# The last token pair of a fused attention and ReGLU kernel: half tiles stored as they complete, and the last product copied by two engines

## The chip, the cores and the metric

The kernel runs on 1 core of one Trainium2 chip, as one program. The metric is the device time of that program in microseconds; lower is better. A change of time is read from medians of several runs.

## The reference

Sigmoid attention (no softmax) over 8 batches, 12 heads, 448 tokens and 64 dimensions is followed by a gated feed-forward layer over the 3584 tokens. The model width is 768, the hidden width 1536, and inputs and output are float32:

```python
def _attn_ref(q, k, v):
    S = q.shape[2]
    scale = 1.0 / np.sqrt(q.shape[-1])
    scores = scale * np.matmul(q, k.transpose(0, 1, 3, 2)) - np.log(S)
    attn = 1.0 / (1.0 + np.exp(-scores))
    return np.matmul(attn, v).astype(np.float32)

def _moe_ref(x, w_gate, w_val, w_out):
    gate = np.maximum(x @ w_gate, 0.0)
    val = x @ w_val
    return (gate * val @ w_out).astype(np.float32)

# x is attention's output with the heads side by side: (8 * 448, 768)
```

## The kernel before

The work is in float16 with float32 accumulation. Batches are taken in pairs (four groups g of two batches, 896 tokens each). The attention of one batch runs between pieces of the feed-forward layer of earlier batches; behind the last batch, the rest of the last group's feed-forward layer stands alone. It ends with the down projection, hidden 1536 to width 768.

The order of the instructions on each engine is the order of the program text (`manual_schedule`). The framework puts in the semaphores between engines. A queue issues in order: an instruction that waits holds up all that stand behind it on the same engine, DMA issues included.

The down projection takes the 896 tokens of a group as seven tiles of 128. One tile goes through `down`, plainly; the other six go in three pairs through `down_pair`. A pair's 256 x 1536 by 1536 x 768 product is treated as a 2 x 2 block product and worked out with seven block products of Strassen's kind instead of eight. `product` is one of them: six matmuls of 128 x 128 by 128 x 384 that sum up in one accumulator tile. There are three accumulator tiles for a pair, b (named "u" in the profile), c ("y12") and a ("y11"), and b takes four of the seven products, one after the other or added to what it holds.

Each product is read by one engine. `scaled_act` copies it on ScalarE (line 421), times OUT_SCALE; `scaled` does that on VectorE (line 416); `plus` adds it, scaled, to what an output tile holds, on VectorE (line 437). The outputs are two SBUF tiles of 128 tokens x 768 float32, y1 and y2 ("ysb"), each with a left half `lo` (columns 0 to 383) and a right half `hi` (384 to 767). HM is 384 and DM is 768.

`store` writes columns m0 to m1 of such a tile to the output, in two DMAs of 64 rows, since the 64-row halves of a tile belong to different chunks of tokens; `engines` names the queue that issues each. Line 339 is the DMA issue. A DMA of all 768 columns carries 192 KB, one of a half tile 96 KB. Only SyncE and ScalarE issue stores, and SyncE does no other work in this stage.

In the last pair (`last`), the order behind the fourth product is: y1's left half is summed; y2's right half is summed; y1's right half is summed; y1 is stored, its first 64 rows by SyncE and its second by ScalarE; the seventh product is made; ScalarE copies it to y2's left half; then y2's right half is stored by SyncE (two DMAs), and its left half by SyncE and ScalarE. The last `scaled_act` and ScalarE's store of y1 are on the same queue, with the store first. `then` has no work left to prepare at that point.

Of the kernel before, what the change touches and what calls it, by code (L numbers as in the profile page):

```python
# [12 lines left out]
AOP = mybir.AluOpType  # L13
AF = mybir.ActivationFunctionType
# [3 lines left out]
def kernel(  # L18
# [10 lines left out]
    nc = tc.nc  # L29

    B, H, S, D = q.shape
    DM, DF = moe_w_gate.shape
# [13 lines left out]
    OUT_SCALE = 1.0 / (XSCALE * XSCALE)  # L46
# [29 lines left out]
    def bank(name, shape=(P, 512), dtype=FP32):  # L76
        pool, tag = free[0]
        free.rotate(-1)
        return pool.tile(list(shape), dtype, tag=tag, name=name)
# [4 lines left out]
    def later(order):  # L84
        keys = [free[i - 8] for i in order]
        for key in keys:
            free.remove(key)
            free.append(key)
# [245 lines left out]
    def store(g, t, ysb, m0, m1, engines):  # L334
        for i, eng in enumerate(engines):
            j = 2 * t + i
            b, c = 2 * g + j // NCH, j % NCH
            dst = out[b * S : (b + 1) * S, m0:m1].rearrange("(t c) m -> c t m", c=NCH)[c]
            eng.dma_start(dst, ysb[64 * i : 64 * i + 64, m0:m1])
# [24 lines left out]
    HF, HM, HD = NFC // 2, DM // 2, NDC // 2  # L364
# [17 lines left out]
    def products(jobs):  # L382
        for ps, n, kn, A, W, first in jobs:
            for k_ in range(kn):
                nc.tensor.matmul(  # L385
                    ps[:, 0:n],
                    A[:, k_, :],
                    W[:, k_, :],
                    start=(first and k_ == 0),
                    stop=(k_ == kn - 1),  # L390
                    skip_group_check=True,
                )
# [8 lines left out]
    def token_blocks(g, p):  # L401
        h = hT_tiles[g]
        t1, t2 = (slice(t * P, (t + 1) * P) for t in (2 * p, 2 * p + 1))
        return h[:, 0:HF, t1], h[:, HF:NFC, t1], h[:, 0:HF, t2], h[:, HF:NFC, t2]
# [15 lines left out]
    def scaled_act(o, ps):  # L420
        nc.scalar.activation(o, ps[:, 0:HM], AF.Copy, scale=OUT_SCALE)  # L421

    def down_pair(g, p, beside, then, last, first_copy):
        A11, A12, S3, A22 = token_blocks(g, p)
        S1, S2, S4 = sums.pop(("y", g, p))
        T1, T2, T3, T4 = (late["T"][:, i] for i in range(4))
        B11, B21, B22 = wo[:, 0:HF, 0:HM], wo[:, HF:NFC, 0:HM], wo[:, HF:NFC, HM:DM]
        y1, y2 = (ysbp.tile([P, DM], FP32, tag="ysb", name="ysb") for _ in range(2))
        lo, hi = slice(0, HM), slice(HM, DM)
        b, c, a = bank("u"), bank("y12"), bank("y11")  # L430
        later((7, 6, 5))

        def product(ps, A, W, first=True):
            products([(ps, HM, HF, A, W, first)])

        def plus(o, ps):
            nc.vector.scalar_tensor_tensor(  # L437
                out=o, in0=ps[:, 0:HM], scalar=OUT_SCALE, in1=o, op0=AOP.mult, op1=AOP.add
            )

        product(b, A11, B11)
        first_copy(y1[:, lo], b)
        beside()
        product(c, S1, T1)
        scaled_act(y2[:, hi], c)
        product(b, S2, T2, False)
        scaled_act(y1[:, hi], b)
        product(a, A12, B21)
        plus(y1[:, lo], a)
        product(b, S3, T3, False)  # L450
        plus(y2[:, hi], b)
        product(c, S4, B22, False)
        plus(y1[:, hi], c)
        if last:
            store(g, 2 * p, y1, 0, DM, (nc.sync, nc.scalar))
        else:
            store(g, 2 * p, y1, 0, DM, (nc.sync, nc.sync))
        then()
        product(b, A22, T4, False)
        scaled_act(y2[:, lo], b)  # L460
        if last:
            store(g, 2 * p + 1, y2, HM, DM, (nc.sync, nc.sync))
            store(g, 2 * p + 1, y2, 0, HM, (nc.sync, nc.scalar))
        else:
            store(g, 2 * p + 1, y2, 0, DM, (nc.sync, nc.sync))


# [199 lines left out]
    def next_work(jobs=(), alone=False):  # L667
        kind, g, i = work.popleft()

        def beside():  # L670
            for job in jobs:
                job()

        if kind == "y":
            down_pair(g, i, beside, prepare, not work, scaled_act if alone else scaled)
        elif kind == "w":
            gv_pair(g, i, lambda: (prepare(), beside()), nc.scalar.copy if alone else nc.vector.tensor_copy)
        else:
            beside()
            prepare()  # L680
            down(g, i)
# [113 lines left out]
```

## Time and profile before

| what | us |
|---|---|
| median of 3 runs | 401.06 (400.89 to 401.36) |
| span of the profiled execution, first to last instruction | 399.2 |
| median of the runs less that span | 1.9 |
| TensorE busy, in the profiled execution | 388.9 (97% of the span) |
| VectorE busy | 279.9 (70%) |
| ScalarE busy | 223.0 (56%) |
| end of the last product, by the timeline | 393.84 |
| issue of the last store, by the timeline | 395.72 |

The profile is one execution; its own time is known by its span, and what lies around the span is taken from the median of the runs. Times in the views are microseconds from the start of the span. PE is TensorE, DVE is VectorE, ACT is ScalarE, SP is SyncE; a q behind an engine's name is its queue's own work, such as issuing a DMA. A row of the timeline gives start, duration, engine, line, operation and what it writes and reads. The time of a DMA issue is that in which the queue is taken; the time to landing runs from the start of the issue to the moment when all of its bytes have been confirmed.

### The profile page before, as it was taken

Reading aid. Unit: us, or ns where it says so; the run is one execution under the profiler, and the core shown is the slowest. Engines: PE = TensorE matmul, PEld = TensorE weight load, DVE = VectorE, ACT = ScalarE, POOL = GpSimd, SP = SyncE. Lnnn points to the kernel's source line nnn. Section 1 sums busy time; section 2 is a strip of 40 time slices with the busy share of each in tenths; the row PEclk is TensorE's granted clock in tenths of the full one; section 3 lists DMA queues with packets and bytes.
Section 4 is the critical chain, followed back from the end, with each engine's and each line's share of the span. In section 5 each row is a group of like instructions: output and inputs, shape, how many; then the busy total and the mean of one; then the engine's idle time right before and its main releaser. Section 6 shows DMA issues by size and latency. Waiting matters only on the chain.

```text
span 399.2 us, 8737 instructions
## 1 busy us (share of the span) xinstructions
PE 388.9 (97%) x3488; PEld 217.9 (55%) x3488; DVE 279.9 (70%) x539; ACT 223.0 (56%) x475; POOL 49.4 (12%) x73
## 2 busy tenths in 40 slices
PE   8999999999998999999999999999999999999994
PEld 3678786545455554554555555455455555555562
DVE  2454344367358889999758889999766779887661
ACT  5946778783885565655665455565566234533131
POOL 8643301600030300003000300000000000000000
PEclk9999999999999999999999999999999999999999
DMA  9999994999897894224945695223012320000144
GB/s 149 199 199 204 205 141 94 177 203 187 178 161 152 165 204 76 46 48 51 178 85 133 130 218 89 48 24 61 12 40 80 80 79 2 0 2 0 39 115 124
DMA packets 68793, 43.69 MB, mean 109 GB/s; under 512 B 35856, under 2 KB 65296, under 8 KB 68752
## 3 DMA queue, kind: packets, MB, share of 16 engines
q0 software_dynamic: 30736, 23.33, 39.1%
q1 hardware_dynamic: 37584, 19.24, 23.0%
q8 instruction: 27, 0.44, 0.5%
q10 hardware_dynamic: 432, 0.56, 0.4%
q14 instruction: 14, 0.11, 0.1%
HBM read 47.19 MB, written 11.01 MB: 146 GB/s over the span
## 4 chain that ended last, share of the span: by engine, by line
PE 73%; DMA 14%; issue 6%; POOL 3%; DVE 2%; ACT 1%; ACTq 0%; POOLq 0%; DVEq 0%
PE u L385 32%; PE g L385 15%; PE y L385 9%; DMA v<-in_v_dram 6%; PE qk_ps L232 5%; PE pv_ps L250 5%; DMA wo<-in_moe_w_out_dram 4%; DMA k<-in_k_dram 4%; PE ya L346 3%; PE v_ps L309 1%; PE yb L346 1%; PE g_ps L309 1%; POOL q L110 1%; POOL k L110 1%; DVE wv L376 1%
## 5 line engine op out<-in xcount | busy, mean ns | idle before, releaser
L187 ACT ACTIVATE PT<-qk_ps 128x448 f16<-128x448 f32 (+3 forms) x318 | 150.6, 594 | 71.2 <-PE qk_ps L232 71.1
L385 PEld LDWEIGHTS <-S 128*128 128x128 f16 x540 | 52.8, 98 | 44.4 <-issue 0.8
L528 DVE TENSOR_TENSOR gsb<-g,gsb 128x448 f32<-128x448 f32 x72 | 43.0, 625 | 14.5 <-PE g L385 13.8
L232 PE MATMUL qk_ps<-qkT 64*64 64x448 f16 (+2 forms) x756 | 50.0, 336 | 0.9 <-DVE qkT L206 0.5
L421 ACT ACTIVATE ysb<-u 128x384 f32<-128x384 f32 x27 | 13.4, 498 | 56.3 <-PE u L385 56.3
L327 DVE TENSOR_TENSOR hT<-gate_sb,v_ps 128x256 f16<-128x256 f32 (+2 forms) x36 | 16.2, 465 | 33.5 <-ACT gate_sb L318 22.4
L385 PEld LDWEIGHTS <-hT 128*128 128x128 f16 x288 | 27.7, 98 | 21.0 <-issue 3.2
L524 ACT COPY gsb<-u 128x448 f32<-128x448 f32 x48 | 25.8, 566 | 23.9 <-PE u L385 22.9
L250 PE MATMUL pv_ps<-PT,v 64*64 64x448 f16 (+2 forms) x756 | 37.4, 329 | 0.4 <-issue 0.4
L184 DVE TENSOR_SCALAR xT<-pv_ps 128x448 f16<-128x448 f32 (+2 forms) x53 | 27.9, 567 | 13.4 <-PE pv_ps L250 12.1
L232 PEld LDWEIGHTS <-qkT 64*64 64x64 f16 x756 | 20.3, 105 | 24.9 <-issue 16.3
L309 PE MATMUL v_ps<-xT,wv 128*128 128x256 f16 (+2 forms) x216 | 33.3, 291 | 0.4 <-DVE hT L327 0.2
L309 PE MATMUL g_ps<-xT,wg 128*128 128x256 f16 (+2 forms) x216 | 33.5, 292 | 0.1
L385 PEld LDWEIGHTS <-wv 128*128 128x128 f16 x216 | 21.1, 98 | 19.8
L385 PEld LDWEIGHTS <-wg 128*128 128x128 f16 x216 | 20.3, 98 | 20.6 <-issue 3.0
L250 PEld LDWEIGHTS <-v 64*64 64x64 f16 x756 | 21.8, 107 | 11.8 <-issue 1.4
L385 PE MATMUL u<-T,hT 128*128 128x384 f16 x144 | 27.3, 326 | 0.0
L437 DVE SCALAR_TENSOR_TENSOR ysb<-y,ysb 128x384 f32<-128x384 f32 x24 | 13.4, 557 | 18.8 <-PE y L385 11.3
L110 POOL DMA_DIRECT2D k<-in_k_dram x14 | 10.9, 779 | 112.3 <-DVE rel L215 105.8
L309 PEld LDWEIGHTS <-wg 128*128 128x128 f16 x216 | 18.5, 98 | 11.5 <-issue 5.0
L309 PEld LDWEIGHTS <-wv 128*128 128x128 f16 x216 | 20.1, 98 | 8.2 <-DMA wv<-in_moe_w_val_dram 0.5
L385 PE MATMUL u<-xT,wg 128*128 128x448 f16 x108 | 23.5, 353 | 0.1
(67 smaller groups left out, 531.3 us busy)
## 6 DMA issues: line engine op xcount, KB each, us to landing
out_dram<-ysb SPq DMA_DIRECT2D x53, 192.0 KB, 2.9
k<-in_k_dram POOLq DMA_DIRECT2D x5, 672.0 KB, 11.8
q<-in_q_dram POOLq DMA_DIRECT2D x5, 672.0 KB, 14.9
v<-in_v_dram POOLq DMA_DIRECT2D x8, 336.0 KB, 15.6
v<-in_v_dram POOLq DMA_DIRECT2D x16, 168.0 KB, 15.3
k<-in_k_dram POOLq DMA_DIRECT2D x8, 224.0 KB, 10.4
wo<-in_moe_w_out_dram POOLq DMA_DIRECT2D x1, 1536.0 KB, 13.2
q<-in_q_dram POOLq DMA_DIRECT2D x6, 224.0 KB, 11.3
```

What stands on the lines that cost most here:

```text
L110: nc.gpsimd.dma_start(t16[:, xs, cs], rows_of(src, b)[:, xs, cs])
L184: nc.vector.tensor_scalar(out=xT, in0=src, scalar1=XSCALE, scalar2=None, op0=AOP.mult)
L187: nc.scalar.activation(PT_ap, ps_ap, AF.Sigmoid, bias=sig_bias, scale=qk_scale)
L232: nc.tensor.matmul(out_of(hh)[o : o + 64, :], qkT[rows, c, cols], qkT[rows, NCH + c0 : NCH + c1, cols], start=True, stop=True, tile_positi ...
L250: nc.tensor.matmul(ps[hh][64 * r : 64 * r + 64, 0:qn], v16[rows, 2 * g + hh, c * D : (c + 1) * D], pieces[c][rows, hh, :], start=(c == 0), ...
L309: nc.tensor.matmul(ps[-1][:, 0:qn], wt[:, dc, f * P : (f + 1) * P], xT_tiles[b][:, dc, q0 : q0 + qn], start=(dc == 0), stop=(dc == NDC - 1),)
L327: nc.vector.tensor_tensor(out=hT_tiles[g][:, f, o : o + qn], in0=gate_sb[:, 0:qn], in1=ps[1][:, 0:qn], op=AOP.mult,)
L346: nc.tensor.matmul(ps[:, 0 : m1 - m0], hT_tiles[g][:, f, t * P : (t + 1) * P], wo[:, f, m0:m1], start=(f == 0), stop=(f == NFC - 1),)
L385: nc.tensor.matmul(ps[:, 0:n], A[:, k_, :], W[:, k_, :], start=(first and k_ == 0), stop=(k_ == kn - 1), skip_group_check=True,)
L421: nc.scalar.activation(o, ps[:, 0:HM], AF.Copy, scale=OUT_SCALE)
L524: by(gs[u][i][:], ps[u][:, 0:S])
L528: nc.vector.tensor_tensor(out=gs[u][i][:], in0=ps[u][:, 0:S], in1=gs[u][i][:], op=AOP.add)
```

## The change

In the last pair alone, three things change. Each half of y1 and the right half of y2 is stored right behind the `plus` that completes it: y1's left half and y2's right half by SyncE, y1's right half by SyncE and ScalarE. The stores of the last pair become eight of 96 KB, six on SyncE and two on ScalarE; before they were two of 192 KB and four of 96 KB. And the seventh product's 384 columns are copied as two quarters of the output tile, columns 0 to 191 by ScalarE and 192 to 383 by VectorE. Nothing else is changed.

```diff
         product(a, A12, B21)
         plus(y1[:, lo], a)
+        if last:
+            store(g, 2 * p, y1, 0, HM, (nc.sync, nc.sync))
         product(b, S3, T3, False)
         plus(y2[:, hi], b)
+        if last:
+            store(g, 2 * p + 1, y2, HM, DM, (nc.sync, nc.sync))
         product(c, S4, B22, False)
         plus(y1[:, hi], c)
         if last:
-            store(g, 2 * p, y1, 0, DM, (nc.sync, nc.scalar))
+            store(g, 2 * p, y1, HM, DM, (nc.sync, nc.scalar))
         else:
             store(g, 2 * p, y1, 0, DM, (nc.sync, nc.sync))
         then()
         product(b, A22, T4, False)
-        scaled_act(y2[:, lo], b)
         if last:
-            store(g, 2 * p + 1, y2, HM, DM, (nc.sync, nc.sync))
+            q3 = slice(0, HM // 2), slice(HM // 2, HM)
+            nc.scalar.activation(y2[:, q3[0]], b[:, q3[0]], AF.Copy, scale=OUT_SCALE)
+            nc.vector.tensor_scalar(
+                out=y2[:, q3[1]], in0=b[:, q3[1]], scalar1=OUT_SCALE, scalar2=None, op0=AOP.mult
+            )
             store(g, 2 * p + 1, y2, 0, HM, (nc.sync, nc.scalar))
         else:
+            scaled_act(y2[:, lo], b)
             store(g, 2 * p + 1, y2, 0, DM, (nc.sync, nc.sync))
```

## The prediction

> **What bounds the kernel now.** I read the page first, for the bound of the whole span.
>
> ```profile
> span 399.2 us, 8737 instructions
> PE 388.9 (97%) x3488; PEld 217.9 (55%) x3488; DVE 279.9 (70%) x539; ACT 223.0 (56%) x475; POOL 49.4 (12%) x73
> ```
>
> TensorE is busy for 97% of the span, and the diff touches none of its instructions. What can move lies behind the last matmul. The chain of waits, asked for the last microseconds, shows what that is (start us, us, what):
>
> ```profile
> 391.89 0.99 PE y L385 x6
> ...
> 392.98 0.57 DVE ysb L437
> ...
> 393.56 0.55 ACTq L339
> 394.11 0.05 issue
> 394.16 0.49 ACT ysb L421
> ```
>
> The last product runs beside the DVE row (the timeline has it from 392.70 to 393.84). ScalarE could then copy it, but it issues a store first (393.56, 0.55 us), so its copy runs from 394.16 to 394.65. The chain stops at that copy; the span goes on to 399.2. So next I read the timeline of SyncE in narrow windows, one store in each:
>
> ```profile
> 393.56 0.47 SPq L339 DMA_DIRECT2D out_dram<-ysb  x1
> 394.07 0.60 SPq L339 DMA_DIRECT2D out_dram<-ysb  x1
> 394.71 0.91 SPq L339 DMA_DIRECT2D out_dram<-ysb  x1
> 395.72 0.54 SPq L339 DMA_DIRECT2D out_dram<-ysb  x1
> ```
>
> This is the bound of the tail. Four stores stand in a row on one queue: one half of the token rows of y1, two of the right half of y2 (complete since 392.54, as DVE's row at 391.99 of 0.56 us says), and the last product's. The copy was done at 394.65, and the last store waits 1.07 us more for its turn. ScalarE's own last store starts at 394.68. The DMA view from 391.0 to 399.2 tells what follows (40 slices of 0.205 us; then KB of each store and us to landing, where the 3.1 is a median):
>
> ```profile
> DMA  0000000000000000028998799899787940000000
> out_dram<-ysb SPq DMA_DIRECT2D x3, 96.0 KB, 3.1
> out_dram<-ysb SPq DMA_DIRECT2D x1, 192.0 KB, 2.7
> out_dram<-ysb ACTq DMA_DIRECT2D x1, 192.0 KB, 3.4
> out_dram<-ysb ACTq DMA_DIRECT2D x1, 96.0 KB, 2.8
> ```
>
> Asked store by store, the three 96 KB ones of SyncE take 3.1, 3.2 and 2.4 us in that order. So the last lands at 395.72 + 2.4 = 398.1, and the span ends 1.1 us behind it, with the program's closing steps. Bytes move from about 394.6 (1.1 us after the first issue) to 397.7 (0.4 us ahead of the last landing). SyncE's store before these was issued by 389.1 (388.53, 0.60 us); from there to 393.56 its queue stands empty, though y1's left half is complete at 391.57 (DVE's row at 391.01, 0.56 us).
>
> The median of the runs is 401.06 us, the profiled span 399.2. I carry the 1.9 us between them unchanged and set the sum against the landing at 398.1.
>
> **The change part by part.**
>
> *Early stores.* Six issues on SyncE replace four, all of 96 KB. Their price on that queue is the issue time. The nearest rows are the four stores of an earlier pair, which stand in one burst:
>
> ```profile
> 379.91 0.47 SPq L339 DMA_DIRECT2D out_dram<-ysb  x1
> 380.42 0.60 SPq L339 DMA_DIRECT2D out_dram<-ysb  x1
> 381.12 0.55 SPq L339 DMA_DIRECT2D out_dram<-ysb  x1
> 381.71 0.59 SPq L339 DMA_DIRECT2D out_dram<-ysb  x1
> ```
>
> With the gaps between them that is about 0.6 us a store; before's 96 KB ones took 0.60, 0.91 and 0.54, so the size does not shorten the issue. Laid end to end: y1 left at 391.59 and 392.10 (queue free at 392.70); y2 right, complete at 392.54, at 392.80 and 393.39 (free at 393.99); y1 right, complete at 393.54, at 394.08 (free at 394.63). Two issues are added, 1.2 us, and they cost nothing while the matmuls to 393.84 and the copies behind them cover them. Without that cover they would push the last store back by 1.2 us. So four of the six are issued by 394.0, and only y1's right half stands ahead of the last store. That one moves from 393.56 to 394.08 on this queue, and only the end of the program waits for it.
>
> *ScalarE's queue.* It still issues y1's store first (half of it), waiting for the same DVE row. I take 0.55 us again, so its copy still starts at 394.16. Between bounds: SyncE issues at the same time, and where both queues issued at once, one store took 0.91 instead of about 0.55. At worst the copy starts 0.36 us later; as ScalarE's two issues measured 0.55 and 0.50 beside a busy SyncE, I take none of it.
>
> *The split copy.* The durations are in the groups by shape, on the same engines:
>
> ```profile
> L318 ACT ACTIVATE gate_sb<-g_ps 128x192 f32<-128x192 f32 x12 | 3.9, 388 | 4.3 <-PE g_ps L309 4.3
> L184 DVE TENSOR_SCALAR xT<-pv_ps 128x192 f16<-128x192 f32 x6 | 1.9, 353 | 2.1 <-PE pv_ps L250 2.1
> ```
>
> The ScalarE mean is 388 ns in a crowded stretch, and one alone at 53.89 takes 0.33 us. As the 128x384 copy is 0.49 in the tail and 0.50 on average, I take 0.33: ScalarE ends at 394.49. For VectorE I take 0.35. It is free from 393.54, and it starts 0.1 us after a matmul's end (391.99 after 391.89), so side by side it would run from 393.94 to 394.29 and cost nothing. The other bound is one after the other: both halves lie in one accumulator tile, and VectorE then starts at about 394.53 and ends at 394.88. The trace does not tell: in the code each product has exactly one reader, so no row has two engines in one bank. I take one after the other, as all rows do, with the ends kept: copies complete at 394.49 or 394.88, where before it was 394.65. Taken so, the split alone is a loss of 0.23 us. The Trainium skill ("PSUM — Partial Sum Buffer", section "PSUM bank collisions raise a hardware error") speaks against this edit: two engines must not be in the same bank and quadrant at once, two readers included, and software has to order them. By that rule the copies end at 394.88, without it at 394.49, and no run here shows a collision.
>
> *The last stores.* VectorE's half makes both of them wait for two engines. Nothing is queued behind either but the closing steps. SyncE is free at 394.63, so both issue at about 394.91: SyncE's 0.81 us earlier than 395.72, ScalarE's 0.23 us later than 394.68. Now SyncE's turn no longer decides, the copies do.
>
> *The landing.* The rows for 96 KB are 2.4 to 3.2 us. The two high ones had two or more stores waiting ahead of them. Of the lowest, 2.4, some was still waiting: a store that waits for nothing has 1.1 us to its first bytes, about 0.4 us of bytes (two slices) and 0.4 us to the landing, 1.9 us. The highest that I allow for is ScalarE's 2.8, with another queue's stores ahead of it. As two stores start together and y1's may still be moving, I take 2.4, and 1.9 to 2.8 as bounds.
>
> *The sum.* 394.91 + 2.4 = 397.31 against 398.1: 0.8 us. The closing steps stay, 1.1 us. SyncE begins them with short waits, one landing after another (L790's rows show eleven of 28 ns in all); up to 0.1 us of them may already be done when the last store lands, and I count 0.05. Together 0.85 us, 401.06 - 0.85 = 400.2 us. The bounds of this case: 1.9 us gives 396.8, a gain of 1.3 (399.75); 2.8 us and ScalarE's copy 0.36 late gives 398.1, no gain (401.05).
>
> **The rivals.**
>
> *Side by side indeed.* The copies end at 394.49; SyncE's queue is then the bound with 394.68, landing 397.1, a gain of 1.0 and 400.0 us; with the 1.9 us landing 1.5, 399.55. For it: VectorE has nothing to do from 393.54. Against: no row shows it.
>
> *The DMA engines hold the tail.* Eight groups of 64 rows replace six with the same bytes. If each takes 0.6 us as on the issuing queue, bytes from 391.59 + 1.1 = 392.7 end at 397.5, the landing is 397.9 and the gain 0.2: 400.85 us. For it: halving the bytes from 192 to 96 KB did not shorten an issue. Against: in before six stores moved from 394.6 to 397.7, 0.52 each, and eight of those end at 396.8.
>
> *Writes wait for the stores (slower).* Each tile is now read by a store while its other half is still to be written. If that write is made to wait until the store has landed, VectorE's last sum of y1 waits at 392.98 for the second store, 392.10 + 3.1 = 395.2. VectorE ends at 395.8, ScalarE issues to 396.4, copies to 396.75 (y2's stores, from 393.39 + 3.1 = 396.5, hold it no longer than that), VectorE's half follows to 397.1, stores land at 397.15 + 2.4 = 399.55: 1.45 us later than 398.1, 402.5 us. It decides once VectorE's sum starts over 0.8 us late, at about 393.8. Against it: before's store of y2's right half started at 394.07, while ScalarE wrote the left half of that tile from 394.16 to 394.65, so halves are told apart in that direction. The opposite direction has no row.
>
> **How the numbers follow.** A change of 0.2%, 0.8 us, is about what a measurement of this kernel can tell from none. My forecast case (copies in turn, stores early) has 0.62; its centre, 0.85, lies just over that mark, so 0.34 of it is faster and 0.28 the same. Side by side has 0.16, all faster. The DMA engines' case has 0.13, the same. Waiting writes have 0.09: 0.07 slower, and 0.02 the same where the wait is short. Together 0.50 faster, 0.43 same, 0.07 slower. The range goes from the lower end of side by side (399.6) to no gain (401.1); what it leaves out is mostly the waiting writes. The forecast case alone has 399.75 to 401.05.
>
> **What would show it.** Right: SyncE stores from 391.6 on with no gap until 394.6; the last pair of stores at about 394.9, landing near 397.3; VectorE's 128x192 row starting only when ScalarE's ends. Wrong: VectorE's row at 393.94 (side by side), a landing time of the last stores of 3 us (the DMA engines), VectorE's sum L437 later than 393.0 or a ScalarE issue of 0.9 us.

## The result and the profile after

| | us |
|---|---|
| before, median of 9 runs | 401.06 (400.78 to 401.75) |
| changed, median of 9 runs | 400.35 (399.83 to 401.10) |
| ratio, 95% interval | 0.9978 [0.9969, 0.9987] |
| predicted | 400.2 (399.6 to 401.1) |

The changed kernel is faster by 0.22%, with the interval from 0.13% to 0.31%. The chain of waits of the changed kernel, in its last microseconds (start us, us, what):

```profile
393.80 0.55 ACTq L339
394.35 0.05 issue
394.40 0.34 ACT ysb L466
394.74 0.02 issue
394.76 0.36 DVE ysb L467
```

ScalarE still issues its store of y1 first, and its copy starts when that is done. VectorE's quarter (L467) starts when ScalarE's has ended. The two copies stand one behind the other.

SyncE's timeline, in narrow windows with one store in each:

```profile
391.83 0.47 SPq L339 DMA_DIRECT2D out_dram<-ysb  x1
392.34 0.60 SPq L339 DMA_DIRECT2D out_dram<-ysb  x1
393.03 0.55 SPq L339 DMA_DIRECT2D out_dram<-ysb  x1
393.63 0.60 SPq L339 DMA_DIRECT2D out_dram<-ysb  x1
394.33 0.54 SPq L339 DMA_DIRECT2D out_dram<-ysb  x1
395.14 0.47 SPq L339 DMA_DIRECT2D out_dram<-ysb  x1
```

In before the queue was taken from 393.56 to 396.26 with four stores in a row. Now five of the six stores are issued by 394.87, and from there the queue is free until both quarters are copied, at 395.12. The DMA view from 391.0 to 398.6 (40 slices of 0.19 us), and the last two stores asked for alone:

```profile
DMA  7000000000696299188549698892789810000000
out_dram<-ysb SPq DMA_DIRECT2D x1, 96.0 KB, 2.2
out_dram<-ysb ACTq DMA_DIRECT2D x1, 96.0 KB, 2.4
```

The first slice still shows the stores ahead of the last pair. The last pair's bytes move from 393.0 on, so while the last product is being made, and they end at about 397.2.

One thing has to be taken out before two single executions are compared. The diff touches nothing ahead of the last pair, yet the last product ends at 393.84 in the profile of before and at 394.07 in this one; in all profiles of this case that end lies between 393.65 and 394.78. This scatter is larger than the effect. What the change does is therefore read from the last product's end to the end of the span: 5.31 us in before, 4.45 us here, 0.86 us less.

### The profile page after: what moved, and what is told of

It is laid out like the page before. It is cut to its first block, busy times and chain, and to the rows that moved or that the text cites. A ratio compares the mean times of both kernels' runs of the same rounds, so it can differ in the third digit from the quotient of the medians.

```text
span 398.5 us, 8744 instructions
## 1 busy us (share of the span) xinstructions
PE 388.5 (97%) x3488; PEld 217.6 (55%) x3488; DVE 280.2 (70%) x540; ACT 222.9 (56%) x475; POOL 49.5 (12%) x73
## 4 chain that ended last, share of the span: by engine, by line
PE 84%; DMA 10%; POOL 2%; DVE 2%; ACT 1%; issue 1%; ACTq 0%; POOLq 0%; DVEq 0%
PE u L385 32%; PE g L385 15%; PE y L385 9%; PE qk_ps L232 7%; PE pv_ps L250 7%; DMA wg<-in_moe_w_gate_dram 6%; PE g_ps L309 5%; PE v_ps L309 5%; DMA v<-in_v_dram 4%; PE ya L346 3%; PE yb L346 1%; POOL q L110 1%; ACT PT L187 1%; DVE wv L376 1%; POOL k L110 1%
```

## The experiments

The theory: in before, SyncE's turn decided when the last store was issued; the early stores empty that queue and bring the gain; the split copy is a small loss, since its halves follow one another. The first rival: the split brings the gain. The second: the DMA engines' pace, not the issue, sets the last landing.

All times of this table are counted from the end of the last product, from the trace. "Issue" is the start of the last store on ScalarE's and on SyncE's queue, "landing" the later landing of the two, "end" the end of the span. Each row's times are of one execution; the two executions of the changed kernel, and the two of e6, agree within 0.03 us.

| kernel | issue ScalarE, SyncE | landing | end | ratio to before, 95% interval |
|---|---|---|---|---|
| before | 0.84, 1.88 | 4.27 | 5.31 | 1 |
| changed | 1.08, 1.07 | 3.49 | 4.45 | 0.9978 [0.9969, 0.9987] |
| after_again | 1.07, 1.07 | 3.46 | 4.42 | 0.9985 [0.9977, 0.9994] |
| e1_early_only | 0.84, 0.89 | 3.44 | 4.34 | 0.9982 [0.9973, 0.9992] |
| e2_split_only | 1.08, 1.88 | 4.54 | 5.57 | 1.0008 [1.0000, 1.0017] |
| e3_y2_first | 0.83, 0.83 | 3.85 | 4.96 | 0.9996 [0.9987, 1.0005] |
| e4_eight_late | 0.84, 1.57 | 3.87 | 4.77 | 0.9990 [0.9981, 0.9998] |
| e5_dve_copy | 0.63, 0.89 | 3.37 | 4.28 | 0.9977 [0.9967, 0.9988] |
| e6_two_queues | 0.63, 0.62 | 3.00 | 3.99 | 0.9962 [0.9949, 0.9976] |
| e6_again | 0.63, 0.62 | 3.00 | 3.97 | 0.9961 [0.9948, 0.9974] |
| e7_vector_first | 0.79, 0.89 | 3.30 | 4.20 | 0.9966 [0.9953, 0.9980] |
| e8_by_rows | 1.43, 0.89 | 3.54 | 4.44 | 0.9979 [0.9970, 0.9988] |
| e9_hi_first | 0.84, 3.00 | 5.16 | 6.06 | 1.0016 [1.0006, 1.0026] |
| e10_two_queues_scalar | 0.79, 0.78 | 3.16 | 4.15 | 0.9974 [0.9964, 0.9984] |

The difference in "end", divided by 401, agrees with every ratio to within its interval (changed: 0.86 / 401 = 0.21%; e9: 0.74 / 401 = 0.18% slower). The intervals are 0.17% wide or wider, which is 0.7 us; where two kernels lie closer than that, the ratios hardly part them, and the comparison rests on single traces.

**The changed kernel again**, on the chip of the next three:

> The changed kernel once more on the same chip, as the measure for the others: ratio to before 0.998, last stores 1.07 us after the last product's end, last landing 2.4 us later.

The same tail to within 0.04 us; the ratio's interval reaches 0.9994 and overlaps the first one. Over both measurements the gain is 0.15 to 0.22%.

**One part alone: the early stores.** The diff is against the changed kernel.

```diff
-            q3 = slice(0, HM // 2), slice(HM // 2, HM)
-            nc.scalar.activation(y2[:, q3[0]], b[:, q3[0]], AF.Copy, scale=OUT_SCALE)
-            nc.vector.tensor_scalar(
-                out=y2[:, q3[1]], in0=b[:, q3[1]], scalar1=OUT_SCALE, scalar2=None, op0=AOP.mult
-            )
+            scaled_act(y2[:, lo], b)
```

> The stores of the change, but ScalarE alone copies the last product (384 columns, 0.49 us). Theory (SyncE's queue was the bound, and the split is a loss because its halves run one after the other): the copy ends about 0.2 us earlier than in the changed kernel, both last stores issue about 0.8 us after the end of the last product instead of 1.07, and the time is 0.2 us below the changed kernel's: a ratio to before of about 0.9973. Rival 'the split brings the gain': the time falls back towards before, ratio 1.000. Rival 'the DMA engines hold the tail': the last landing does not move although the last stores issue earlier, ratio equal to the changed kernel's, 0.998.

The tail keeps all of its gain without the split (4.34 us), so the first rival is out. The last stores issue when the theory said, 0.2 us ahead of the changed kernel, but the landing comes only 0.01 to 0.05 us earlier; the rest of the 0.08 to 0.11 us at the end is in the closing steps (0.90 us instead of 0.96). SyncE's last store now takes 2.56 us instead of 2.17. The last two stores, asked for alone:

```profile
out_dram<-ysb ACTq DMA_DIRECT2D x1, 96.0 KB, 2.4
out_dram<-ysb SPq DMA_DIRECT2D x1, 96.0 KB, 2.6
```

So the second rival has a part in it; e8 and e10 below take that up.

**The other part alone: the split copy**, with before's stores in before's order.

```diff
-        scaled_act(y2[:, lo], b)
         if last:
+            q3 = slice(0, HM // 2), slice(HM // 2, HM)
+            nc.scalar.activation(y2[:, q3[0]], b[:, q3[0]], AF.Copy, scale=OUT_SCALE)
+            nc.vector.tensor_scalar(
+                out=y2[:, q3[1]], in0=b[:, q3[1]], scalar1=OUT_SCALE, scalar2=None, op0=AOP.mult
+            )
             store(g, 2 * p + 1, y2, HM, DM, (nc.sync, nc.sync))
             store(g, 2 * p + 1, y2, 0, HM, (nc.sync, nc.scalar))
         else:
+            scaled_act(y2[:, lo], b)
```

> The split copy alone; the stores are those of before, in before's order. Theory: nothing is gained, since SyncE's last store comes to its turn about 1.88 us behind the last product's end either way; ScalarE's last store is 0.2 us later and lands before SyncE's. Ratio 1.000, within 0.0005; VectorE's row starts when ScalarE's has ended. Rival 'the split brings the gain': ratio 0.998, with both rows at the same time.

SyncE's last store issues at 1.88 us, as before, so the split gains nothing. It even loses 0.26 us, which I had not expected. SyncE's timeline, and the landing of that one store:

```profile
396.27 0.59 SPq L339 DMA_DIRECT2D out_dram<-ysb  x1
out_dram<-ysb SPq DMA_DIRECT2D x1, 96.0 KB, 2.7
```

In before the same store took 2.4 us. ScalarE's store, 0.24 us later than in before because of the serial copies, now moves its bytes closer to SyncE's last ones (it lands at 4.18 instead of 3.60 us behind the product). That the two get in each other's way is what the times suggest; it was not tried by itself.

**Order of the queue alone.** Six stores as in before, but y2's right half goes ahead of y1, which is stored whole; ScalarE copies the last product whole.

```diff
         plus(y2[:, hi], b)
+        if last:
+            store(g, 2 * p + 1, y2, HM, DM, (nc.sync, nc.sync))
         product(c, S4, B22, False)
...
         if last:
-            store(g, 2 * p + 1, y2, HM, DM, (nc.sync, nc.sync))
             store(g, 2 * p + 1, y2, 0, HM, (nc.sync, nc.scalar))
```

> Only the order of the queue: y2's right half is stored when it is complete instead of behind y1, y1 is stored whole as before, ScalarE copies the last product whole. Six stores, as in before. Theory (turn on the queue): SyncE is free when the copy is done, the last stores issue about 0.8 us after the last product instead of 1.88, ratio 0.997 to 0.998. Rival 'the DMA engines hold the tail': y1's two 192 KB stores now move bytes up to the end, the last stores take 3 us or more to land and half of the gain is lost, ratio 0.9985 or above. Rival 'splitting y1 is what matters': ratio near 1.000.

The last stores issue at 0.83 us, 1.05 us earlier than in before, and yet the end comes only 0.36 us earlier. Their landings, asked for alone:

```profile
out_dram<-ysb SPq DMA_DIRECT2D x1, 96.0 KB, 2.8
out_dram<-ysb ACTq DMA_DIRECT2D x1, 96.0 KB, 3.0
```

Here the second rival holds. Y1's two stores of 192 KB are issued just ahead, land at 2.54 and 3.15 us behind the product, and the last ones queue behind them. Turning the queue round was not enough; y1's left half has to be away early as well.

**Y1 in halves, meant to be late.**

```diff
         if last:
-            store(g, 2 * p, y1, 0, DM, (nc.sync, nc.scalar))
+            store(g, 2 * p, y1, 0, HM, (nc.sync, nc.sync))
+            store(g, 2 * p, y1, HM, DM, (nc.sync, nc.scalar))
```

> Before with y1 stored in halves, but no earlier than before: two more issues stand on SyncE's queue in the tail, uncovered, and the bytes are the same. Theory (each issue costs its 0.6 us on the queue once nothing covers it): the last store issues about 1.2 us later than in before, ratio 1.002 to 1.003. Rival 'bytes set the tail': same bytes, same time, ratio 1.000.

The edit did not do what I meant. SyncE's timeline:

```profile
392.40 1.11 SPq L339 DMA_DIRECT2D out_dram<-ysb  x2
```

This is 2.25 us ahead of the last product's end (394.65 in this run). SyncE has no other work, so a store's place in the program text does not hold it; it issues as soon as its half tile is complete and the stores ahead of it on the same queue are gone. So this run is "y1's left half early, y2's right half still behind y1": 0.54 us of gain. With e3's 0.36 us for y2's order, and 0.97 us for both (e1), each early half has a share.

**The issues without cover.** The same stores with y1's right half ahead of its left one, so that SyncE has to wait for y1's last sum first:

```diff
         if last:
-            store(g, 2 * p, y1, 0, DM, (nc.sync, nc.scalar))
+            store(g, 2 * p, y1, HM, DM, (nc.sync, nc.scalar))
+            store(g, 2 * p, y1, 0, HM, (nc.sync, nc.sync))
```

> Before with y1 stored in halves, the right half first and the left half behind it, so that no store of the tail can issue before y1's last sum: eight stores, none of them covered by the last products, the bytes as in before. Theory (an issue costs its 0.6 us on SyncE's queue once nothing covers it): the last store issues 2.8 to 3.1 us behind the end of the last product instead of 1.88, and the span ends 6.2 to 6.5 us behind it instead of 5.3: ratio 1.002 to 1.003. Rival 'bytes set the tail': same bytes at the same time, 5.3 us, ratio 1.000.

```profile
397.50 0.55 SPq L339 DMA_DIRECT2D out_dram<-ysb  x1
out_dram<-ysb SPq DMA_DIRECT2D x1, 96.0 KB, 2.2
```

The last store issues 3.00 us behind the product (394.50 in this run), 1.12 us later than in before: the price of two issues that nothing covers, with the same bytes. Only 0.74 us of that reach the end (6.06 us, a little less than expected), since the store that is alone at the end lands in 2.2 instead of 2.4 us and the closing steps take 0.90 instead of 1.04. "Bytes alone set the tail" is out.

**Who orders the two copies.** First by rows instead of columns, 64 rows for each engine; the diff is against the changed kernel:

```diff
-            q3 = slice(0, HM // 2), slice(HM // 2, HM)
-            nc.scalar.activation(y2[:, q3[0]], b[:, q3[0]], AF.Copy, scale=OUT_SCALE)
-            nc.vector.tensor_scalar(
-                out=y2[:, q3[1]], in0=b[:, q3[1]], scalar1=OUT_SCALE, scalar2=None, op0=AOP.mult
-            )
+            nc.scalar.activation(y2[0:64, lo], b[0:64, 0:HM], AF.Copy, scale=OUT_SCALE)
+            nc.vector.tensor_scalar(
+                out=y2[64:P, lo], in0=b[64:P, 0:HM], scalar1=OUT_SCALE, scalar2=None, op0=AOP.mult
+            )
```

> The stores of the change; the last product is shared out by rows, 0 to 63 to ScalarE and 64 to 127 to VectorE, 384 columns each. If two engines are kept apart only where they share rows of the accumulator, VectorE runs from 0.1 to 0.65 us after the last product, beside ScalarE (0.3 to 0.8), and the last stores issue at 0.7 (ScalarE's queue) and 0.85 us: ratio 0.997. If they are kept apart by the accumulator as a whole, VectorE starts when ScalarE ends, at 0.85, and the last stores issue at 1.45 us: 0.4 us above the changed kernel, ratio 0.999.

```profile
394.95 0.48 ACT L465 ACTIVATE ysb<-u 64x384 f32<-64x384 f32 x1 [3.70 <-PE u L385]
395.47 0.56 DVE L466 TENSOR_SCALAR ysb<-u 64x384 f32<-64x384 f32 x1 [1.15 <-ACT ysb L465]
```

VectorE's 64 other rows wait for ScalarE all the same, and the row names ScalarE as what ended its wait. Half the rows take as long as all (0.48 and 0.56 us), so the copies end at 1.40 us. The time I expected for this case was wrong: SyncE's store only needs ScalarE's rows and issues at 0.89, and ScalarE's, issued at 1.43, lands in 2.11 us. The end is that of the changed kernel. The two copies share the accumulator and the output tile, and the row does not say which of them is guarded. The output tile is told apart by rows at least between a copy and a store: SyncE's store of rows 0 to 63 issues at 0.89, while VectorE writes rows 64 to 127 from 0.84 to 1.40. That points to the accumulator, but no run copies one accumulator to two output tiles.

The landings of e8's last two stores also bear on e1:

```profile
out_dram<-ysb SPq DMA_DIRECT2D x1, 96.0 KB, 2.3
out_dram<-ysb ACTq DMA_DIRECT2D x1, 96.0 KB, 2.1
```

SyncE's store has the same issue time as in e1, 0.89 us, and the same stores ahead of it on its queue. ScalarE's last store differs: it comes 0.54 us behind SyncE's here, and 0.05 us ahead of it in e1. SyncE's lands in 2.30 us here and in 2.56 us in e1. (In e7 and e5, where ScalarE's is 0.10 and 0.26 us ahead, it takes 2.41 and 2.48 us.) So some 0.26 us of e1's landing goes with ScalarE's store, started just ahead; the stores on SyncE's own queue, the same in both, do not explain it.

Then the two quarters in the opposite order of text:

> The change with the two quarter copies in the opposite order of text, VectorE's first. If the order of text decides who waits, VectorE runs from 0.04 to 0.40 us behind the last product and ScalarE from 0.43 to 0.76; ScalarE's store issues at 0.79, SyncE's at its turn, 0.89, and the span ends 4.3 us behind the product instead of 4.45. If ScalarE's copy goes first whatever the text says, nothing changes: 1.07 and 4.45 us.

```profile
394.82 0.36 DVE L466 TENSOR_SCALAR ysb<-u 128x192 f32<-128x192 f32 x1 [0.35 <-PE u L385]
395.21 0.33 ACT L469 ACTIVATE ysb<-u 128x192 f32<-128x192 f32 x1 [3.80 <-DVE ysb L466]
```

Now VectorE goes first and ScalarE waits, 0.43 us behind the product. The order of the text decides who waits. This way round is better, since VectorE's quarter fills the time in which ScalarE issues its store: the copies end at 0.76 instead of 1.04 us and the span ends 0.22 to 0.25 us earlier than in the changed kernel.

**VectorE alone copies**, with the stores of the change; the short diff is against e1:

```diff
-            scaled_act(y2[:, lo], b)
+            scaled(y2[:, lo], b)
```

> The stores of the change; VectorE alone copies the last product (384 columns, 0.56 us), with ScalarE left to its store. Theory: VectorE starts 0.1 us after the last product, as ScalarE's 0.3 us delay by its store is gone; the copy ends 0.65 us after the product, ScalarE's store follows at once and SyncE's when its queue is free, at about 0.85. 0.2 us below the changed kernel: ratio 0.997. If SyncE's turn is the bound again it is no better than the early stores with ScalarE's copy.

The copy ends at 0.59 us, 0.22 earlier than ScalarE's, but SyncE's turn comes at 0.89 in both, and the end is 0.06 us better than e1's. SyncE's queue is the bound again.

**Both queues, and the pace of the landings.** Each half tile is stored by SyncE and ScalarE. First with ScalarE's copy; the diff is against e1:

```diff
-            store(g, 2 * p, y1, 0, HM, (nc.sync, nc.sync))
+            store(g, 2 * p, y1, 0, HM, (nc.sync, nc.scalar))
...
-            store(g, 2 * p + 1, y2, HM, DM, (nc.sync, nc.sync))
+            store(g, 2 * p + 1, y2, HM, DM, (nc.sync, nc.scalar))
```

> Each half tile is stored by SyncE (64 rows) and ScalarE (64 rows) when it is complete, and ScalarE copies the last product whole. The last stores issue 0.84 us behind the last product, as they do with the early stores on SyncE alone and ScalarE's copy (0.84 and 0.89). If the stores still moving on SyncE's queue stretched the landing there (2.56 us), it falls to 2.15 to 2.4 here and the span ends 4.15 to 4.2 us behind the product instead of 4.34. If the time of the last issue alone counts, it ends at 4.3 again.

The last stores issue 0.06 to 0.11 us earlier than e1's, and the landing comes 0.28 us earlier: 2.14 us (SyncE) and 2.38 us (ScalarE) instead of 2.56 and 2.35:

```profile
out_dram<-ysb SPq DMA_DIRECT2D x1, 96.0 KB, 2.1
out_dram<-ysb ACTq DMA_DIRECT2D x1, 96.0 KB, 2.4
```

The stores now come in pairs that issue 0.97 us or more apart. SyncE's take 2.12 to 2.16 us and ScalarE's 2.37 to 2.38 us in every pair, so no pair waits behind another. This confirms the time that was expected, but not the reason by itself, since two things change at once: SyncE's queue has no store close ahead of the last one, and SyncE's last store no longer starts behind ScalarE's. By e8 the second is worth some 0.26 us of the 0.41 us that SyncE's landing falls, and about 0.15 us is left for the first. In the changed kernel, where the last two also start together, SyncE's takes 2.17 us, issued 0.18 us later than in e1 behind the same stores.

Then with VectorE's copy (`scaled`) as well, meant to beat both kernels:

> Meant to beat both: each half tile is stored by SyncE (64 rows) and ScalarE (64 rows) when it is complete, and VectorE copies the last product. Theory: both queues are empty when the copy ends, 0.65 us after the last product, so the last stores issue at 0.7 us instead of 1.07 (changed kernel) and 1.88 (before): ratio 0.9965 to 0.997. Rival 'the DMA engines hold the tail': the last stores take longer to land by what they issue earlier, ratio 0.998 as in the changed kernel.

> Half tiles stored by both queues, VectorE copying the last product, once more, for a narrower interval: ratio to before 0.9955 to 0.9975, and the span ends 4.0 us behind the last product.

The last two stores of e6_again, by the timeline and the DMA view, where the product ends at 393.82:

```profile
394.44 0.47 SPq L339 DMA_DIRECT2D out_dram<-ysb  x1
394.44 0.50 ACTq L339 DMA_DIRECT2D out_dram<-ysb  x1
out_dram<-ysb SPq DMA_DIRECT2D x1, 96.0 KB, 2.2
out_dram<-ysb ACTq DMA_DIRECT2D x1, 96.0 KB, 2.4
```

Both issue as soon as the copy is done. The medians are 399.80 and 399.83 us beside 401.19 and 401.33 for before on the same chips, the ratios 0.9962 and 0.9961. In the trace the tail is 1.33 us shorter than before's, 0.47 us of that beyond the changed kernel. It has the shortest tail and the lowest ratio of all kernels tried here, though several intervals overlap with its own.

## Why the prediction was right

- **The bound.** SyncE's turn, read from its four stores in a row, was what held the last store. E1 (early stores alone, 0.97 us off the tail) and e9 (the same number of stores without cover, 0.74 us onto it) show both directions.
- **The issues end to end.** Counted from the product's end, the forecast had SyncE's stores at -2.25, -1.74, -1.04, -0.45, 0.24 and 1.07 us; they came at -2.25, -1.73, -1.04, -0.44, 0.26 and 1.07. The gaps of an earlier burst of the same trace were the right rows for that. The cover was real: uncovered, two more issues delayed the last one by 1.12 us (e9), where I had said 1.2.
- **The copies.** ScalarE at 0.32 to 0.65 as forecast, VectorE at 0.69 to 1.04 as forecast; durations 0.33 and 0.36 us for 0.33 and 0.35. That they run one after the other was taken as the cautious one of two bounds, as no row had two engines in one bank. E2 and e8 show that it is so, for separate rows too, and e7 that the order of the text decides who goes first. The Trainium skill ("PSUM — Partial Sum Buffer", section "PSUM bank collisions raise a hardware error") says that different quadrants of one bank may be used at once; in e8 the program's own wait kept even those apart, so what the chip would have done is not shown by any run. VectorE, going first, started 0.04 us after the product (e5, e6, e7), not 0.1.
- **The landing.** 2.4 us was taken; the two last stores took 2.17 and 2.42. That this comes out to 0.02 us is partly luck: the 2.4 was the time of SyncE's last store in before, and SyncE's took 2.17 here; the later landing is ScalarE's. Of the two reasons given, that two stores start together held: in e6 and e10 ScalarE's takes 2.37 to 2.39 us beside SyncE's. That y1's stores may still be moving added little here. The lower bound of 1.9 us, pieced together from slices, was too low: the lowest 96 KB store of any run took 2.08 us, the first one of the tail, with no store of the last pair ahead of it (e1, e5). Bytes were counted too short: in the changed kernel the first store's take three slices of the DMA row, about 0.6 us, and not 0.4.
- **The closing steps.** 0.05 us of gain allowed, 0.08 measured (1.04 to 0.96). Over all kernels these steps take 0.90 to 1.11 us, so a difference of this size says little. SyncE's eleven short rows of L790 take 17 to 28 ns each, not 28 all.
- **The sum.** 0.85 us forecast; 0.86 us in the tail of the profile, and 0.71 us between the medians of 9 runs; 0.85 us, or 0.21%, lies within the interval. That the time fell is clear of noise. Whether it fell by more than the 0.2% at which the forecast parted "faster" from "same" is not settled: both intervals of the changed kernel contain that mark.
- **The rivals.** Side by side did not happen. Writes did not wait for the stores: VectorE's last sum starts 0.87 us ahead of the product's end in before and after alike. The DMA engines' pace was given too little: it did not decide the change, but in e1 the last stores issue 0.2 us earlier and the later landing gains 0.05 us at most, and in e3 two thirds of the earlier issue are lost again. My statement that the split alone costs 0.23 us was for the issue time; at the end of the span it costs 0.26 us with before's stores (e2) and 0.1 us with the early ones (e1 against the changed kernel).

## What to carry to other kernels

The end of a kernel is a chain of its own: list the issues of each queue behind the last matmul, since a queue that issues in order can hold the last store back long after its data is ready. Send what is complete early and over both queues, so that at the end only the last tile's stores are left and nothing is still landing ahead of them. Splitting a copy over two engines gave no overlap here, where both halves lie in one accumulator: the copies ended at 1.04 us with ScalarE first, at 0.76 with VectorE first and at 0.59 with VectorE alone. Give the copy, or at least its first part, to the engine whose queue has nothing else in front.

## What was not expected of the hardware

- In the last pair an issue takes the queue 0.47 to 0.60 us whether it carries 96 or 192 KB (both have 64 rows), with four exceptions: 0.91 us for SyncE's third store in before and in e2, 0.69 us in e4 and 0.74 us in e9. What stretches these is not shown; in e1 an issue at the same moment, with ScalarE's queue also storing, takes 0.54 us.
- Of two 96 KB stores that start together on the two queues, SyncE's lands after 2.12 to 2.18 and ScalarE's after 2.37 to 2.39 us, in all pairs of e6 and e10. With 192 KB stores just ahead (e3) it is 2.82 and 3.02 us.
- The last product's end, ahead of which nothing differs, scatters over 1.1 us between single profiles, more than the 0.86 us of the change.
